# Fixed order and an earlier wait for the first loads of two batches, and a plan with later landings

## The chip, the cores and the metric

The kernel runs on one core of a Trainium2 chip. The metric is the device time of one execution in microseconds (us). A single profiled execution says where time goes, and is itself one draw. Each execution comes with a state, fast or slow (over 1.5% above the fastest of the same kernel, for a kernel on one core).

Names: TensorE (PE in the profile; PEld is its weight load), VectorE (DVE), ScalarE (ACT), GpSimd (POOL), and SyncE (SP), which only issues transfers here. A queue name such as SPq is the engine's instruction queue.

## The reference

Two stages, cut to the mathematics:

```python
# attention: 8 batches, 8 heads, 576 tokens, head size 64, float32
phi(x) = concat(relu(x) * cos_w, relu(x) * sin_w)          # 128 features
kv  = einsum('bhsf,bhsd->bhfd', phi(k), v);  z = phi(k).sum(over s)
num = einsum('bhsf,bhfd->bhsd', phi(q), kv)
den = einsum('bhsf,bhf->bhs', phi(q), z)[..., None] + 1e-6
x   = (num / den)   # as 4608 tokens x 512
# two layers: w_in 512 x 2048, w_out 2048 x 512
h = x @ w_in;  g = h * cos(h);  out = g @ w_out
```

## The kernel before

One Python class, `Plan`, collects steps (engine, cost, data read and written), guesses when each will run, and emits the instructions of each engine in the order of that guess. On the chip the order is fixed and every engine takes its instructions one after the other. A bad guess of when data land therefore makes an engine stand at an instruction whose data are late, with ready work behind it.

The guess for transfers, in the class (cut):

```python
    SHARE, WAKE, LAND = {"HW": 0.42, "SW": 0.58}, {"HW": 1.1, "SW": 1.6}, 1.0
    ...
                for r in on:                    # rings HW (issued by SyncE) and SW (by GpSimd)
                    if rings[r][0][1] < 1e-6:
                        n = rings[r].pop(0)[2]
                        done[n] = now + self.LAND
    ...
                rings[r].append([free[e] + self.WAKE[r], s["dma"][0] / s["dma"][1], n])
```

The transfers of the start. A batch's k, q and v come as float32 through SyncE. The weights come through GpSimd and are cast to float16 on the way. A tiny GpSimd copy (a "hold") that reads one buffer and writes a few elements of another is how one transfer is made to wait for another:

```python
    def weights():
        # hold: w_in waits for batch 0's k
        pl.add("POOL", 0.4, 0.5, 0, hold, hk("k"), [("w_in", g) for g in range(4)])
        for g in range(4):
            ...                                 # w_in, quarter g
        # hold2: w_out waits for w_in's second quarter
        pl.add("POOL", 0.2, 0.3, 0, hold2, [("w_in", 1)], [("w_out", g) for g in range(4)])
        w_out_load(0, 2)                        # first half of w_out

    def hold_raw(nm):                           # batch 1's loads wait for w_out's first quarter
        pl.add("POOL", 0.2, 0.3, 0, lambda: nc.gpsimd.tensor_copy(
            out=raw[nm][0:2, 0, 0, 0:1], in_=w_out_sb[0:2, 0, 0:1]),
            [("w_out", 0)], [((nm, 0), 0), ((nm, 0), 1)])

    def rest_of_w_out():                        # second half of w_out waits for batch 1's q
        ...
        pl.add("POOL", 0.2, 0.3, 0, hold, hk("q"), [("w_out", g) for g in (2, 3)])
        w_out_load(2, 4)

    def second_attention():
        T = start[1] - 30
        for nm, hs in (("k", (slice(0, H),)), ("q", (slice(0, H),)), ("v", HALVES)):
            hold_raw(nm)
            load(1, nm, T, hs)
            if nm == "q":
                rest_of_w_out()
        ...
```

v is loaded in two halves of the heads, but the hold writes only head 0: v's second half is not guarded.

The end of the start-up, in the words used below. Batch 0 goes through attention and layer 1. Then batch 1's attention runs: for each of five groups of tokens a numerator on TensorE, a division on VectorE, a transpose on TensorE, a copy. This is a serial chain. What fills TensorE between its links is layer 2 of batch 0, in eight **filler blocks** of eight 128x512 matmuls, 1.73 us each (`layer2_plain`): four need w_out's first half, four its second. Layer 1 of batch 1 follows.

```python
    def layer2_plain(c):
        ...
        for jh in range(2):                     # half of w_out
            for n, t in enumerate(range(NT) if jh == 0 else (3, 2, 0, 1)):
                ...
                pe(JH, MM, due, mm, [...] + [("w_out", 2 * jh), ("w_out", 2 * jh + 1)], [mk])
```

## Time and profile before

| | before |
|---|---|
| median of the first three executions | 297.37 us (297.03 to 297.64) |
| span of the profiled execution | 295.5 us |
| TensorE issues without a gap from | 140.8 us to 291 us |
| batch 1's hold on GpSimd | 29.0 us |
| first layer-1 matmul of batch 1 | 60.2 us |

Lines of the page of the kernel before. The second and third line cut the span into 40 slices of 7.4 us; a digit is the busy share of TensorE, or its granted clock, in tenths. The last line is the chain that ended last, by engine.

```profile
span 295.5 us, 6280 instructions
...
PE   6768998699999999999999999999999999999994
...
PEclk9977999999999999999999999999999999999999
...
PE 67%; DMA 15%; DVE 9%; ACT 5%; issue 2%; SPq 0%; ACTq 0%; DVEq 0%
```

TensorE is full from the ninth slice on. What can be won lies before it, and the chain names transfers as 15% of the time. The windows view shows where: start and end, length, then busy time and count by engine, the granted clock, the share of the transfer engines and GB/s.

```profile
14.00:26.30 12.30, 8.43 (x105) 6.28 (x103) 7.42 (x28) 5.59 (x12) 1.67 (x3) 0.72 1.21 223
...
42.00:60.00 18.00, 13.41 (x160) 8.48 (x159) 13.58 (x34) 12.06 (x20) 0.00 (x0) 1.00 1.00 259
60.00:141.00 81.00, 79.36 (x773) 57.83 (x771) 76.77 (x160) 62.63 (x103) 0.00 (x0) 1.00 0.96 231
```

From 42 to 60 us TensorE is busy for 13.41 of 18 us: a hole. In the waits view, from 14 to 62 us (us in total, times, longest), these are the waits for late data:

```profile
ACT V L329 <- DMA vm<-in_v_dram: 3.2, 1, 3.2
...
DVE V L332 <- DMA vm<-in_v_dram: 2.9, 1, 2.9
...
DVE kp L319 <- DMA km<-in_k_dram: 2.0, 1, 2.0
...
ACT kp L316 <- DMA km<-in_k_dram: 1.2, 1, 1.2
```

The first two are the unguarded half of v, at 21 to 24 us; the others are batch 2's k, at 51 to 53 us. The timeline of GpSimd: start, length, instruction; in brackets its idle time before and what ended it as far as the profile sees.

```profile
16.19 0.19 POOL L695 COPY w_out_sb<-w_in_sb 1x4 f16<-1x4 f16 x1 [2.93 <-DMA w_in_sb<-in_moe_w_in_dram]
...
29.03 0.18 POOL L708 CAST km<-w_out_sb 2x1 f32<-2x1 f16 x1 [10.87 <-ACT ch L464]
```

The second is batch 1's hold. It waits for w_out's first quarter (the engine named last is only the latest of several that it waits for). The timeline of TensorE over the hole:

```profile
47.14 0.43 PE L404 MATMUL ATT<-kvz,qT 128*128 128x65 f16 x8 [0.79 <-DVE qT L378]
...
47.86 1.89 PE L553 MATMUL M<-w_out_sb,gT 128*128 128x512 f16 x8
49.58 0.42 PE L404 MATMUL ATT<-kvz,qT 128*128 128x65 f16 x8
...
51.22 0.42 PE L404 MATMUL ATT<-kvz,qT 128*128 128x65 f16 x8 [0.33 <-DVE x L424]
52.01 0.38 PE L444 MATMUL M<-IDENT,x 128*128 128x128 f16 x4 [0.37 <-ACT qT L376]
54.69 0.38 PE L444 MATMUL M<-IDENT,x 128*128 128x128 f16 x4 [2.29 <-DVE qT L378]
54.91 1.89 PE L553 MATMUL M<-w_out_sb,gT 128*128 128x512 f16 x8
...
59.75 0.62 PE L444 MATMUL M<-IDENT,x 128*128 128x128 f16 x8 [0.70 <-DVE x L424]
60.21 1.91 PE L491 MATMUL M<-xT,w_in_sb 128*128 128x256 f16 x16
```

L404 are numerators, L444 transposes, L553 a filler block, L491 layer 1.

One more measure is used below, **lost TensorE time**. Take the matmuls' steps from the trace (0.216 us for 128x512, 0.109 us for 128x256, 0.03 to 0.056 us for the small ones), add those issued up to a moment, and subtract from that moment. The sum over the whole kernel is 268.4 us including warm-up matmuls, the same for every kernel here, so what is lost is what differs. A matmul at half clock counts as half lost. Before loses 14.4 us up to 26.3 us, 0.0 from there to 42, 5.6 from 42 to 60, and 2.3 from 60 to 141 us.

### The profile page before, as it was taken

Reading aid. Unit: us, or ns where it says so; the run is one execution under the profiler, and the core shown is the slowest. Engines: PE = TensorE matmul, PEld = TensorE weight load, DVE = VectorE, ACT = ScalarE, POOL = GpSimd, SP = SyncE. Lnnn points to the kernel's source line nnn. Section 1 sums busy time; section 2 is a strip of 40 time slices with the busy share of each in tenths; the row PEclk is TensorE's granted clock in tenths of the full one; section 3 lists DMA queues with packets and bytes.
Section 4 is the critical chain, followed back from the end, with each engine's and each line's share of the span. In section 5 each row is a group of like instructions: output and inputs, shape, how many; then the busy total and the mean of one; then the engine's idle time right before and its main releaser. Section 6 shows DMA issues by size and latency. Waiting matters only on the chain.

```text
span 295.5 us, 6280 instructions
## 1 busy us (share of the span) xinstructions
PE 276.6 (94%) x2460; PEld 194.4 (66%) x2460; DVE 239.3 (81%) x486; ACT 183.6 (62%) x293; POOL 8.9 (3%) x20
## 2 busy tenths in 40 slices
PE   6768998699999999999999999999999999999994
PEld 2446866268977677666766766676668566666783
DVE  2975786798999899988998999999879858665741
ACT  2945895698987756767386849575544554645320
POOL 1520020000000000000000000000000000000000
PEclk9977999999999999999999999999999999999999
DMA  6999979999956999999999939971925100300304
GB/s 214 322 228 213 289 189 257 310 337 191 273 162 157 182 234 250 230 210 297 215 233 298 265 101 241 231 188 46 143 59 170 41 0 2 142 2 1 123 21 142
DMA packets 77565, 53.27 MB, mean 180 GB/s; under 512 B 46048, under 2 KB 75232, under 8 KB 77536
## 3 DMA queue, kind: packets, MB, share of 16 engines
q1 hardware_dynamic: 72592, 48.12, 63.9%
q0 software_dynamic: 4224, 4.19, 8.7%
q10 hardware_dynamic: 720, 0.57, 0.6%
q8 instruction: 19, 0.31, 0.4%
q14 instruction: 10, 0.08, 0.1%
HBM read 36.74 MB, written 9.44 MB: 156 GB/s over the span
## 4 chain that ended last, share of the span: by engine, by line
PE 67%; DMA 15%; DVE 9%; ACT 5%; issue 2%; SPq 0%; ACTq 0%; DVEq 0%
PE M L613 28%; PE M L509 27%; DMA vm<-in_v_dram 7%; PE M L491 6%; DMA qm<-in_q_dram 6%; DVE gT L466 3%; DMA km<-in_k_dram 3%; PE ATT L404 2%; PE ATT L343 2%; ACT ch L464 2%; DVE x L424 1%; PE M L553 1%; ACT kp L316 1%; ACT qp L316 1%; DVE V L332 1%
## 5 line engine op out<-in xcount | busy, mean ns | idle before, releaser
L464 ACT ACTIVATE ch<-M,PIH 128x512 f32<-128x512 f32 x144 | 97.9, 686 | 60.4 <-PE M L509 57.0
L466 DVE TENSOR_TENSOR gT<-M,ch 128x512 f16<-128x512 f32 x144 | 96.8, 685 | 25.8 <-ACT ch L464 24.9
L509 PE MATMUL M<-xT,w_in_sb 128*128 128x512 f16 x384 | 93.8, 379 | 0.0
L613 PEld LDWEIGHTS <-gT 128*128 128x128 f16 x640 | 62.4, 98 | 18.4 <-issue 1.7
L509 PEld LDWEIGHTS <-w_in_sb 128*128 128x128 f16 x448 | 42.1, 98 | 35.0
L613 PE MATMUL M<-w_out_sb,gT 128*128 128x256 f16 x384 | 46.8, 273 | 1.3 <-ACT ost L624 1.3
L491 PE MATMUL M<-xT,w_in_sb 128*128 128x256 f16 x256 | 31.8, 282 | 1.6 <-ACT xT L448 1.6
L613 PE MATMUL M<-T,S 128*128 128x256 f16 x256 | 32.5, 273 | 0.0
L613 PE MATMUL M<-T,gT 128*128 128x256 f16 x256 | 32.2, 273 | 0.0
L613 PEld LDWEIGHTS <-S 128*128 128x128 f16 x256 | 25.1, 98 | 8.0
L491 PEld LDWEIGHTS <-w_in_sb 128*128 128x128 f16 x256 | 25.5, 101 | 5.9 <-issue 2.1
L316 ACT ACTIVATE qp<-qm,CS 128x512 f16<-128x512 f32 x38 | 25.3, 713 | 6.5 <-DMA qm<-in_q_dram 6.5
L316 ACT ACTIVATE kp<-km,CS 128x512 f16<-128x512 f32 x39 | 26.4, 713 | 1.4 <-DMA km<-in_k_dram 1.4
L424 DVE TENSOR_TENSOR x<-ATT,rec 128x512 f16<-128x512 f32 x33 | 22.8, 691 | 1.1
L319 DVE TENSOR_SCALAR qp<-qm,CS 128x512 f16<-128x512 f32 x42 | 18.7, 484 | 5.7 <-DMA qm<-in_q_dram 5.7
L595 DVE TENSOR_TENSOR S<-gT 128x1024 f16<-128x1024 f16 x32 | 21.6, 685 | 0.2
L319 DVE TENSOR_SCALAR kp<-km,CS 128x512 f16<-128x512 f32 x41 | 18.3, 487 | 2.4 <-DMA km<-in_k_dram 2.4
L404 PEld LDWEIGHTS <-qT 128*128 128x128 f16 x320 | 14.7, 98 | 6.3 <-issue 2.7
L404 PE MATMUL ATT<-kvz,qT 128*128 128x65 f16 x296 | 14.8, 194 | 1.6 <-DVE qT L378 0.8
L509 PE MATMUL M<-xR,w_in_sb 128*128 128x512 f16 x64 | 16.1, 379 | 0.0
L332 DVE CAST V<-vm 128x512 f16<-128x512 f32 (+1 forms) x42 | 13.7, 382 | 2.9 <-DMA vm<-in_v_dram 2.9
L343 PEld LDWEIGHTS <-kp 128*128 128x128 f16 x320 | 10.9, 97 | 2.8 <-ACT V L329 1.1
(66 smaller groups left out, 180.2 us busy)
## 6 DMA issues: line engine op xcount, KB each, us to landing
out_dram<-ost SPq DMA_DIRECT2D x33, 256.0 KB, 3.0
qm<-in_q_dram SPq DMA_DIRECT2D x8, 640.0 KB, 6.4
km<-in_k_dram SPq DMA_DIRECT2D x8, 640.0 KB, 5.9
qm<-in_q_dram SPq DMA_DIRECT2D x8, 512.0 KB, 7.0
km<-in_k_dram SPq DMA_DIRECT2D x8, 512.0 KB, 6.7
vm<-in_v_dram SPq DMA_DIRECT2D x6, 640.0 KB, 5.5
vm<-in_v_dram SPq DMA_DIRECT2D x6, 512.0 KB, 5.5
w_in_sb<-in_moe_w_in_dram POOLq DMA_DIRECT2D x4, 512.0 KB, 10.1
```

What stands on the lines that cost most here:

```text
L316: act(0.12 + 0.5 * f, due, lambda: nc.scalar.activation(out=out_, in_=in_, func=AF.Relu, scale=sc), rd, wr)
L319: dve(0.09 + 0.33 * f, due, lambda: nc.vector.tensor_scalar(out=out_, in0=in_, scalar1=0.0, scalar2=sc, op0=ALU.max, op1=ALU.mult), rd, wr)
L332: dve(0.09 + 0.33 * f, due, lambda: nc.vector.tensor_copy(out=out_, in_=in_), rd, wr)
L343: nc.tensor.matmul(bank[hb][:, hh * D1:(hh + 1) * D1], lhsT=kp[:, t, h].rearrange("p g d -> p (g d)"), rhs=V1[:, t, h, :], start=(t == 0), ...
L404: nc.tensor.matmul(bank[hb][:, hh * D1:(hh + 1) * D1], lhsT=a[:, h, :], rhs=z[:, h, :], start=(i == 0), stop=(i == len(parts) - 1))
L424: nc.vector.tensor_tensor(out=split(x16[n][:, hs, :], k), in0=A[:, :, :, 0:D], in1=split(rec[n][:, hs], k).unsqueeze(3).broadcast_to((P, k ...
L464: act(0.59, due, lambda: nc.scalar.activation(out=ch[c], in_=bank, func=AF.Sin, bias=PIH, scale=1.0), [key, "PIH"], [("ch", c)])
L466: dve(0.61, due, lambda: nc.vector.tensor_tensor(out=dst, in0=bank if len(dst.shape) == 2 else bank.rearrange("p (j s) -> p j s", j=dst.sh ...
L491: nc.tensor.matmul(M1[m][:, jj * 2 * P:(jj + 1) * 2 * P], lhsT=w_in_sb[:, cc, j * P:(j + 1) * P], rhs=X[:, cc, ts], start=(cc == 0), stop= ...
L509: nc.tensor.matmul(M1[m], lhsT=w_in_sb[:, cc, j * P:(j + 1) * P], rhs=X[:, cc, :], start=(cc == 0), stop=(cc == NCT - 1))
L595: dve(0.07 + 1.07 / NG, due, lambda: nc.vector.tensor_tensor(out=out_[:, sl], in0=a[:, sl], in1=b[:, sl], op=op), rd, wr)
L613: nc.tensor.matmul(M2[bank][:, tt * MH:(tt + 1) * MH], lhsT=a[:, j, tt * P:(tt + 1) * P], rhs=b[:, j, :], start=(first and tt == 0 and j = ...
```

## The change

The intent is to let batch 1's data come as soon as the first weights have landed, in a fixed order with nothing that cuts in, and to have the plan believe in later landings so that engines do not stand at late data. Core of the diff (cut; the rest carries the new `lane` argument through the plan's forward and backward passes):

```diff
-    SHARE, WAKE, LAND = {"HW": 0.42, "SW": 0.58}, {"HW": 1.1, "SW": 1.6}, 1.0
+    SHARE, WAKE, LAND = {"HW": 0.40, "SW": 0.56}, {"HW": 1.1, "SW": 1.3}, 1.0
+    BUSY, MARGIN = 2.2, 1.0
...
-                        done[n] = now + self.LAND
+                        if r == "SW" and not rings["SW"]:
+                            for x in rings["HW"]:
+                                x[0] = min(x[0], max(now, x[3]))
+                        done[n] = now + self.LAND + (self.MARGIN if now > 13.0 else 0.0)
...
-                rings[r].append([free[e] + self.WAKE[r], s["dma"][0] / s["dma"][1], n])
+                wake = free[e] + self.WAKE[r]
+                late = wake + (self.BUSY if r == "HW" and rings["SW"] and not rings["HW"] else 0.0)
+                rings[r].append([late, s["dma"][0] / s["dma"][1], n, wake])
...
+    ORDER0, ORDER1, HOLDW = "qkv", "kqv", 1
+    GATE1 = (w_in_sb[0:2, 0, Dff // 2 + 1:Dff // 2 + 2], [("w_in", 2)])
...
-            pl.add("SP", 0.65, 0, due, go4, (), [(x, 1 - n) for x in part], dma=(nb * NT, 355.0))
+            pl.add("SP", 0.65, 0, due, go4, (), [(x, 1 - n) for x in part], dma=(nb * NT, 355.0),
+                   lane="first" if b < 2 else None)
...
     def hold_raw(nm):
-        pl.add("POOL", 0.2, 0.3, 0, lambda: nc.gpsimd.tensor_copy(
-            out=raw[nm][0:2, 0, 0, 0:1], in_=w_out_sb[0:2, 0, 0:1]),
-            [("w_out", 0)], [((nm, 0), 0), ((nm, 0), 1)])
+        for h in (0, HB) if nm == ORDER1[2] else (0,):
+            pl.add("POOL", 0.2, 0.3, 0, lambda h=h: nc.gpsimd.tensor_copy(
+                out=raw[nm][0:2, h, 0, 0:1], in_=GATE1[0]),
+                GATE1[1], [((nm, h), 0), ((nm, h), 1)])
```

So there are four parts: the earlier wait (w_in's third quarter instead of w_out's first), the guard on both halves of v, the fixed load order, and the plan's numbers. What the diff does not tell is that the plan, seeing batch 1 wait for w_in's third quarter, loads that quarter first of the four.

More of the change, by code (lines that the diff above doesn't have):

```diff
@@ L36, in __init__, with add @@
         self.steps = []
-        self.wr, self.rd = {}, {}
-    def add(self, eng, occ, lat, due, fn, rd=(), wr=(), dma=None):
+        self.wr, self.rd, self.lanes = {}, {}, {}
+    def add(self, eng, occ, lat, due, fn, rd=(), wr=(), dma=None, lane=None):
         n = len(self.steps)
+        prev = self.lanes.get(lane)
+        if lane is not None:
+            self.lanes[lane] = n
         deps = set()
@@ L55, in add @@
         self.steps.append(dict(eng=eng, occ=occ, lat=lat, due=due, fn=fn,
-                               deps=deps, dma=dma, n=n))
+                               deps=deps, dma=dma, n=n, prev=prev))
         return n
@@ L85, in forward @@
                 users[d].append(s["n"])
+        follow = {s["prev"]: s["n"] for s in st if s["prev"] is not None}
+        left = [k + (s["prev"] is not None) for k, s in zip(left, st)]
         avail, start, done = [0.0] * len(st), [0.0] * len(st), [0.0] * len(st)
@@ L134, in forward @@
             free[e] = t + s["occ"]
+            if n in follow:
+                u = follow[n]
+                avail[u] = max(avail[u], t)
+                left[u] -= 1
+                if not left[u]:
+                    ready[st[u]["eng"]].append(u)
             if s["dma"] is None:
@@ L149, in backward @@
                 left[d] += 1
+            if s["prev"] is not None:
+                left[s["prev"]] += 1
         limit = [end - done[n] + start[n] for n in range(len(st))]
@@ L171, in backward @@
                 limit[d] = min(limit[d], late[n] - self.link(d, n) - (done[d] - start[d]))
+                left[d] -= 1
+                if not left[d]:
+                    ready[st[d]["eng"]].append(d)
+            d = st[n]["prev"]
+            if d is not None:
+                limit[d] = min(limit[d], late[n] - 0.01)
                 left[d] -= 1
@@ L299, in load @@
             nb = len(part) * R * D * 4 / 1e3
-            pl.add("SP", 0.65, 0, due, go4, (), [(x, 1 - n) for x in part], dma=(nb * NT, 355.0))
-            pl.add("SP", 0.65, 0, due, go5, (), [(x, n) for x in part], dma=(nb * (NT + 1), 355.0))
+            pl.add("SP", 0.65, 0, due, go4, (), [(x, 1 - n) for x in part], dma=(nb * NT, 355.0),
+                   lane="first" if b < 2 else None)
+            pl.add("SP", 0.65, 0, due, go5, (), [(x, n) for x in part], dma=(nb * (NT + 1), 355.0),
+                   lane="first" if b < 2 else None)
     def hk(nm, hs=range(H)):
@@ L686, in hold @@
                 out=w_in_sb[0:1, 0, :].rearrange("p (g f) -> p g f", g=4)[:, :, 0],
-                in_=raw["k"][0:1, 0, 0, 0:1].broadcast_to((1, 4)))
-        pl.add("POOL", 0.4, 0.5, 0, hold, hk("k"), [("w_in", g) for g in range(4)])
+                in_=raw[ORDER0[1]][0:1, 0, 0, 0:1].broadcast_to((1, 4)))
+        pl.add("POOL", 0.4, 0.5, 0, hold, hk(ORDER0[1]), [("w_in", g) for g in range(4)])
         for g in range(4):
@@ L707, in hold_raw, with rest_of_w_out @@
     def hold_raw(nm):
-        pl.add("POOL", 0.2, 0.3, 0, lambda: nc.gpsimd.tensor_copy(
-            out=raw[nm][0:2, 0, 0, 0:1], in_=w_out_sb[0:2, 0, 0:1]),
-            [("w_out", 0)], [((nm, 0), 0), ((nm, 0), 1)])
-    def rest_of_w_out():
+        for h in (0, HB) if nm == ORDER1[2] else (0,):
+            pl.add("POOL", 0.2, 0.3, 0, lambda h=h: nc.gpsimd.tensor_copy(
+                out=raw[nm][0:2, h, 0, 0:1], in_=GATE1[0]),
+                GATE1[1], [((nm, h), 0), ((nm, h), 1)])
+    def rest_of_w_out(nm):
         def hold():
@@ L715, in hold @@
                 out=w_out_sb[0:1, JH:, 0].rearrange("p (g j) -> p g j", g=2)[:, :, 0],
-                in_=raw["q"][0:1, 0, 0, 0:1].broadcast_to((1, 2)))
-        pl.add("POOL", 0.2, 0.3, 0, hold, hk("q"), [("w_out", g) for g in (2, 3)])
+                in_=raw[nm][0:1, 0, 0, 0:1].broadcast_to((1, 2)))
+        pl.add("POOL", 0.2, 0.3, 0, hold, hk(nm), [("w_out", g) for g in (2, 3)])
         w_out_load(2, 4)
@@ L724, in first_attention @@
         warm(14, 6.5)
-        for nm, hs in (("q", (slice(0, H),)), ("k", (slice(0, H),)), ("v", HALVES)):
-            load(0, nm, 0, hs)
+        for nm in ORDER0:
+            load(0, nm, 0, HALVES if nm == ORDER0[2] else (slice(0, H),))
         weights()
@@ L745, in second_attention @@
         T = start[1] - 30
-        for nm, hs in (("k", (slice(0, H),)), ("q", (slice(0, H),)), ("v", HALVES)):
+        for nm in ORDER1:
             hold_raw(nm)
-            load(1, nm, T, hs)
-            if nm == "q":
-                rest_of_w_out()
+            load(1, nm, T, HALVES if nm == ORDER1[2] else (slice(0, H),))
+            if nm == ORDER1[HOLDW]:
+                rest_of_w_out(nm)
         for t in range(NT + 1):
```

## The prediction

> **What bounds it now.** TensorE. In the trace's matmul rows successive starts are 0.216 us apart for 128x512, 0.109 us for 128x256. These steps add up to about 263 us outside the warm-ups, in a span of 295.5. From 141 to 291 us it issues without a gap, from 60 to 110 nearly so. Only the early stages can give time: by the same rows about 2.6 us are lost from 22 to 26.3 us, 5.5 us from 42 to 60, 2.3 us from 70 to 141. The first 14 us (batch 0's loads) stay.
>
> **Why these gaps are there.**
> - The waits view: ScalarE waits 3.2 us and VectorE 2.9 us (to 24.4 us) for batch 1's second half of v, a load without a guard. Issued at 14.8 us, its data moved only from 18.6 to 23.2 us, and delayed w_in. Its cast sits ahead of the first cosine on ScalarE, so layer 1 of batch 0 runs freely only from 26.2 us.
> - Batch 1's k and q wait for w_out's first quarter: GpSimd's hold runs at 29.0 us, data flow from 30.5 to 40 us.
> - Batch 2's k is issued at 40.3 us beside w_out's last half and lands near 53 us; VectorE waits 2.0 us and ScalarE 1.2 us for it, with batch 1's copies behind in their queues. Layer 1 of batch 1 starts at 60.2 us.
>
> **What the change does.** No matmul or byte is added, only one GpSimd hold of 0.17 us. The new instruction order (built, not run) puts w_in's third quarter first on GpSimd. So batch 1's hold comes near 16.2 us instead of 29.0, and k, q, v follow in this order, all guarded; the early v load is gone. w_out's first half is issued near 22 us instead of 16.7.
>
> **Estimate of the transfers.** Packet rows: loads alone move about 360 KB/us, weights alone 205 KB/us (written), together about 125 and 115. This agrees with the Trainium skill, "DMA: Bandwidth & Descriptors", Issuing engines are not separate DMA queues: both interleave on the same 16 engines. A load issued beside weights starts 3 to 4 us late. So: w_in complete near 25 us, batch 1's k near 30, q 36, v 40, w_out near 48 (before 50.5), batch 2's k under 51.
>
> **Critical path.** Layer 1 of batch 0: 1.0 us (only part of that gap, as the granted clock is 0.5 from 18.7 to 25.5 us and the idle stretch before it stays). Batch 1's attention and its filler matmuls: 2.4 us. Better estimates of later landings, fewer stalls from 58 to 141 us: 1 us, uncertain, since VectorE is nearly full there (25.8 of 27 us). Sum 4.4 us; a little off for new stalls: **293.3 us, 290.0 to 297.2**. Chances: faster by over 2% 0.22, within 2% 0.75, slower 0.03.
>
> **What would show it.** The waits for v at 21 to 24 us gone; batch 1's first hold near 16 us; layer 1 of batch 0 continuous from about 21.5 us; waits for batch 2's k below 1 us; layer 1 of batch 1 starting at 55 to 57 us; TensorE without gaps from about 137 us to the end.
>
> **What would make it wrong.** Batch 1's k landing after 33 us would stall ScalarE among the cosines of layer 1. The rest of w_in, or w_out's first half, landing later than its matmuls need, since they now share with k and q. The reordered stretch from 100 to 141 us, where VectorE leads, costing or giving 1 to 2 us.

## The result, and the profile after

| | before | after |
|---|---|---|
| median, first comparison | 297.5 us (4 executions) | 292.77 us (4; 292.04 to 293.85) |
| median, repeated on another chip | 296.81 us (11) | 292.73 us (6; 291.68 to 293.96) |
| span of the profiled execution | 295.5 us | 290.6 us |
| TensorE without a gap from | 140.8 us | 136.0 us |

The ratio of the first comparison is 0.9846 (95% interval 0.9811 to 0.9881), of the second 0.9856 (0.9824 to 0.9888). Ratios and intervals here are from the fast executions of the same rounds. They are close to the ratio of the mean times (the largest difference is 0.0013, in the run of the plan's numbers alone), and not quite the ratio of the medians.

The page of the changed kernel:

```profile
span 290.6 us, 6281 instructions
...
PE   7678998999999999998999999999999999999993
...
PEclk9988999999999999999999999999999999999999
...
PE 84%; DMA 7%; DVE 4%; ACT 3%; issue 1%; SPq 0%; DVEq 0%; ACTq 0%
```

The chain has lost half of its share of transfers. The windows:

```profile
14.00:26.30 12.30, 8.94 (x113) 6.79 (x114) 8.80 (x30) 5.75 (x11) 3.23 (x9) 0.86 1.20 228
...
42.00:60.00 18.00, 16.40 (x197) 11.25 (x195) 15.70 (x39) 15.04 (x26) 0.00 (x0) 1.00 1.07 296
60.00:141.00 81.00, 80.20 (x771) 59.06 (x770) 77.96 (x161) 59.23 (x97) 0.00 (x0) 1.00 0.91 225
```

TensorE is busy for 16.40 instead of 13.41 us between 42 and 60 us. By lost time: 13.6 us up to 26.3 us (before 14.4), 0.0 to 42 us (0.0), 2.7 to 60 us (5.6), 1.3 to 141 us (2.3). The differences, 0.8, 2.9 and 1.0, make 4.7 of the 4.8 us by which the gapless stretch starts earlier.

The waits for late data, from 14 to 62 us:

```profile
ACT kp L346 <- DMA km<-in_k_dram: 1.5, 1, 1.5
...
ACT V L359 <- DMA vm<-in_v_dram: 0.7, 1, 0.7
...
DVE V L362 <- DMA vm<-in_v_dram: 0.4, 1, 0.4
```

The 3 us waits for v at 21 to 24 us are gone; batch 2's k still costs ScalarE 1.5 us. GpSimd: batch 1's first hold, and the hold ahead of w_out.

```profile
17.04 0.18 POOL L739 CAST km<-w_in_sb 2x1 f32<-2x1 f16 x1 [2.20 <-DMA w_in_sb<-in_moe_w_in_dram]
...
23.14 0.19 POOL L725 COPY w_out_sb<-w_in_sb 1x4 f16<-1x4 f16 x1 [5.67 <-DMA w_in_sb<-in_moe_w_in_dram]
```

TensorE where the hole was:

```profile
45.85 0.42 PE L434 MATMUL ATT<-kvz,qT 128*128 128x65 f16 x8
...
47.56 0.42 PE L434 MATMUL ATT<-kvz,qT 128*128 128x65 f16 x8 [0.84 <-DVE x L454]
48.15 1.89 PE L583 MATMUL M<-w_out_sb,gT 128*128 128x512 f16 x8 [0.18 <-DVE gT L496]
49.88 0.42 PE L434 MATMUL ATT<-kvz,qT 128*128 128x65 f16 x8
...
50.58 1.89 PE L583 MATMUL TR<-w_out_sb,gT 128*128 128x512 f16 x8
...
52.79 1.89 PE L583 MATMUL M<-w_out_sb,gT 128*128 128x512 f16 x8
...
55.22 1.89 PE L583 MATMUL TR<-w_out_sb,gT 128*128 128x512 f16 x8
56.95 1.91 PE L521 MATMUL M<-xT,w_in_sb 128*128 128x256 f16 x16
```

A filler block (L583) now stands between the links of the chain about every 2.3 us. Layer 1 of batch 1 starts at 56.95 instead of 60.21 us.

### The profile page after: what moved, and what is told of

The parts are those of the page before. It is cut to its first block, busy times and chain, and to the rows that moved or that the text cites. A ratio compares the mean times of both kernels' runs of the same rounds, so it can differ in the third digit from the quotient of the medians.

```text
span 290.6 us, 6281 instructions
## 1 busy us (share of the span) xinstructions
PE 276.6 (95%) x2460; PEld 194.4 (67%) x2460; DVE 239.6 (82%) x486; ACT 182.8 (63%) x293; POOL 9.0 (3%) x21
## 4 chain that ended last, share of the span: by engine, by line
PE 84%; DMA 7%; DVE 4%; ACT 3%; issue 1%; SPq 0%; DVEq 0%; ACTq 0%
PE M L643 33%; PE M L539 33%; PE M L521 7%; DMA vm<-in_v_dram 4%; PE ATT L434 3%; DMA km<-in_k_dram 3%; PE ATT L373 2%; PE M L583 2%; PE TR L583 1%; DVE x L454 1%; DVE kp L349 1%; ACT qp L346 1%; ACT ch L494 1%; PE M L373 1%; PE M L474 1%
## 5 line engine op out<-in xcount | busy, mean ns | idle before, releaser
L494 ACT ACTIVATE ch<-M,PIH 128x512 f32<-128x512 f32 x144 | 98.2, 686 | 66.5 <-PE M L539 56.4
L346 ACT ACTIVATE qp<-qm,CS 128x512 f16<-128x512 f32 x38 | 25.4, 714 | 4.9 <-DMA qm<-in_q_dram 4.9
L625 DVE TENSOR_TENSOR S<-gT 128x1024 f16<-128x1024 f16 x32 | 21.5, 684 | 0.3
L373 PEld LDWEIGHTS <-kp 128*128 128x128 f16 x320 | 11.7, 97 | 3.9 <-ACT V L359 1.3
```

The lines of the kernel that those rows point to most:

```text
L346: act(0.12 + 0.5 * f, due, lambda: nc.scalar.activation(out=out_, in_=in_, func=AF.Relu, scale=sc), rd, wr)
L373: nc.tensor.matmul(bank[hb][:, hh * D1:(hh + 1) * D1], lhsT=kp[:, t, h].rearrange("p g d -> p (g d)"), rhs=V1[:, t, h, :], start=(t == 0), ...
L494: act(0.59, due, lambda: nc.scalar.activation(out=ch[c], in_=bank, func=AF.Sin, bias=PIH, scale=1.0), [key, "PIH"], [("ch", c)])
L625: dve(0.07 + 1.07 / NG, due, lambda: nc.vector.tensor_tensor(out=out_[:, sl], in0=a[:, sl], in1=b[:, sl], op=op), rd, wr)
```

## The experiments

Theory at the start, T: the data of batch 1 and w_out arrive earlier, which pays about 3.4 us, and the plan's numbers pay about 1 us more. Rival P: the better plan pays. Rival V: taking away the early load of v pays. Each kernel was timed in five rounds beside the kernel before on the same chip; four kernels shared a chip and its executions of before. Every result was correct.

The table holds what each run showed. Columns: the time of batch 1's hold; the last packet of its q and of w_out; the start of its first numerator; how many of the eight filler blocks were already spent by then; lost TensorE time from 26.3 to 42, from 42 to 60 and from 60 to 141 us; median and ratio. "Last packet" is the start of the last packet. All but the last two columns are of the one profiled execution. The loss up to 26.3 us is left out: it is 12.3 to 14.5 us in these 14 executions, and the half clock of the start has part in it. All times are in us.

| kernel | hold | q | w_out | first num. | blocks spent | lost 26-42 | lost 42-60 | lost 60-141 | median | ratio (95%) |
|---|---|---|---|---|---|---|---|---|---|---|
| before | 29.0 | 38.3 | 51.7 | 47.1 | 3 | 0.0 | 5.6 | 2.3 | 296.6 to 297.5 | 1 |
| the change | 17.0 | 36.6 | 47.9 | 45.8 | 2 | 0.0 | 2.7 | 1.3 | 292.77 | 0.9846 |
| plan's numbers only | 29.4 | 39.1 | 55.0 | 46.6 | 4 | 0.0 | 6.9 | 0.4 | 297.53 | 1.0019 (0.9984 to 1.0053) |
| old numbers | 16.9 | 36.3 | 47.6 | 45.2 | 2 | 1.6 | 0.1 | 3.6 | 294.70 | 0.9922 (0.9892 to 0.9952) |
| old wait | 28.1 | 37.5 | 48.4 | 48.4 | 4 | 0.0 | 6.9 | 1.6 | 297.88 | 1.0022 (0.9992 to 1.0052) |
| new wait, old order | 18.2 | 37.3 | 47.6 | 47.6 | 3 | 0.5 | 3.6 | 1.9 | 295.66 | 0.9961 (0.9927 to 0.9994) |
| no margin | 17.0 | 36.5 | 48.2 | 45.4 | 2 | 0.4 | 1.6 | 2.6 | 293.48 | 0.9904 (0.9855 to 0.9954) |
| early v, free order | 18.9 | 39.8 | 50.4 | 48.3 | 3 | 2.7 | 5.0 | 1.0 | 297.88 | 1.0017 (0.9986 to 1.0048) |
| late wait, same order | 25.4 | 40.6 | 53.5 | 49.8 | 2 | 4.3 | 1.9 | 1.5 | 297.31 | 1.0011 (0.9981 to 1.0041) |
| the change again | 17.3 | 36.4 | 47.6 | 46.0 | 2 | 0.0 | 3.1 | 1.3 | 292.73 | 0.9856 (0.9824 to 0.9888) |
| w_out late, same order | 16.8 | 36.2 | 52.9 | 46.9 | 2 | 1.4 | 1.9 | 1.8 | 295.35 | 0.9954 (0.9923 to 0.9984) |
| free order | 17.0 | 40.0 | 53.4 | 46.6 | 2 | 2.3 | 2.8 | 0.1 | 293.68 | 0.9896 (0.9865 to 0.9926) |
| quarters in order | 23.0 | 36.6 | 48.8 | 44.0 | 2 | 0.2 | 1.9 | 3.0 | 293.37 | 0.9890 (0.9861 to 0.9919) |
| margin 2 us | 20.0 | 36.6 | 47.7 | 48.1 | 2 | 2.7 | 1.0 | 0.6 | 293.25 | 0.9885 (0.9857 to 0.9914) |

### Only the plan's numbers

The changed kernel with its three other parts put back (cut; the `lane` argument is taken out at both of its places):

```diff
-    GATE1 = (w_in_sb[0:2, 0, Dff // 2 + 1:Dff // 2 + 2], [("w_in", 2)])
+    GATE1 = (w_out_sb[0:2, 0, 0:1], [("w_out", 0)])
-                   lane="first" if b < 2 else None)
+                   lane=None)
-        for h in (0, HB) if nm == ORDER1[2] else (0,):
+        for h in (0,):
```

> The kernel before with nothing new but the plan's numbers and rules for transfers (shares, wake times, the 2.2 us start beside weights, the 1 us margin); batch 1 waits for w_out's first quarter as before, its second half of v is unguarded again and no load order is fixed. Theory T (the data arrive earlier; the plan's numbers are worth about 1 us): 296 to 297 us, ratio to before 0.996 to 1.000, first hold of batch 1 near 29 us. Rival P (the better plan is what pays): 293 to 294.5 us, ratio 0.985 to 0.990, the waits for batch 2's k at 51 to 53 us gone although the data come as late as before.

Measured: 297.53 us, ratio 1.0019. P falls: a plan that believes in later landings, alone, gains nothing. It spends all four blocks of w_out's first half before the first numerator, and the next block comes at 57.9 us. The profiled execution was the fastest of its six (294.94 us), so its stages flatter it.

### The plan's old numbers

```diff
-    SHARE, WAKE, LAND = {"HW": 0.40, "SW": 0.56}, {"HW": 1.1, "SW": 1.3}, 1.0
-    BUSY, MARGIN = 2.2, 1.0
+    SHARE, WAKE, LAND = {"HW": 0.42, "SW": 0.58}, {"HW": 1.1, "SW": 1.6}, 1.0
+    BUSY, MARGIN = 0.0, 0.0
```

> The changed kernel with the plan's old numbers (no margin, no late start, old shares and wake): the transfers are moved, but planned as optimistically as before. T: 293.5 to 294.5 us, ratio 0.986 to 0.990. P: 296 us or more, ratio above 0.995, with waits of VectorE and ScalarE for late loads between 30 and 60 us of 2 us or more.

Measured: 294.70 us, ratio 0.9922: between the two theories. The hole is gone here too, but 3.6 us are lost after 60 us. This is the timeline of TensorE there, in the kernel with the old numbers:

```profile
69.18 0.43 PE L434 MATMUL ATT<-kvz,qT 128*128 128x65 f16 x8 [0.37 <-DMA qT<-qp]
...
71.61 0.43 PE L434 MATMUL ATT<-kvz,qT 128*128 128x65 f16 x8 [1.12 <-DMA qT<-qp]
```

TensorE itself stands at numerators of batch 2 whose transposed q, another transfer, is late. In the changed kernel no wait of TensorE for a transfer is listed in that stretch.

### The old wait

```diff
-    GATE1 = (w_in_sb[0:2, 0, Dff // 2 + 1:Dff // 2 + 2], [("w_in", 2)])
+    GATE1 = (w_out_sb[0:2, 0, 0:1], [("w_out", 0)])
```

> The changed kernel with one thing put back: batch 1's loads wait for w_out's first quarter. Both halves of v stay guarded, order fixed, new plan numbers. First hold of batch 1 near 27 us (no early v beside w_in), q of batch 1 landing near 37 us instead of 34. T: 294.5 to 296 us, ratio 0.990 to 0.995, about half of the gain lost. P: 293 to 293.5 us, as the changed kernel, since the plan knows of the later data. A third theory V (only the early v and its head-of-line wait matter): also as the changed kernel.

Measured: 297.88 us, ratio 1.0022. The whole gain is gone, where T had expected half, and P and V none. Yet most data are hardly later than in the change: q by 0.9 us, w_out by 0.5. Only k is 4.5 us later (33.8 against 29.3), and this kernel first uses it at 37.8 us. No engine but GpSimd waits for a transfer between 14 and 50 us in this trace. The loss is in the order. TensorE of the kernel with the old wait:

```profile
38.48 1.89 PE L583 MATMUL M<-w_out_sb,gT 128*128 128x512 f16 x8
40.20 1.89 PE L583 MATMUL TR<-w_out_sb,gT 128*128 128x512 f16 x8
41.93 1.89 PE L583 MATMUL M<-w_out_sb,gT 128*128 128x512 f16 x8
...
45.15 1.89 PE L583 MATMUL M<-w_out_sb,gT 128*128 128x512 f16 x8
...
48.38 0.42 PE L434 MATMUL ATT<-kvz,qT 128*128 128x65 f16 x8
...
51.73 0.42 PE L434 MATMUL ATT<-kvz,qT 128*128 128x65 f16 x8 [0.66 <-DVE x L454]
...
53.36 0.60 PE L434 MATMUL ATT<-kvz,qT 128*128 128x65 f16 x8 [0.99 <-DVE x L454]
...
55.18 0.61 PE L474 MATMUL M<-IDENT,x 128*128 128x128 f16 x4 [0.80 <-DVE x L454]
...
56.04 3.60 PE L583 MATMUL M<-w_out_sb,gT 128*128 128x512 f16 x8
```

Told of the later wait, the plan put batch 1's preparation behind nearly all of layer 1 of batch 0, and all four first-half blocks ahead of the first numerator. The chain then runs with no filler block between its links from 48.4 to 56.0 us. Neither the weights nor the gates forced this: the next block needs w_out's second half, whose last packet came at 48.4 us, and gates of batch 0, the last of which VectorE ended at 43.6 us; the block stands in the order at 56.04. It takes 3.60 instead of 1.89 us: after the thin stretch the clock was granted at half from 53.3 to 60.1 us.

### The new wait in the old order

The kernel before, with one source changed; no engine's order moves:

```diff
-            out=raw[nm][0:2, 0, 0, 0:1], in_=w_out_sb[0:2, 0, 0:1]),
+            out=raw[nm][0:2, 0, 0, 0:1], in_=w_in_sb[0:2, 0, Dff // 4 + 1:Dff // 4 + 2]),
```

> The kernel before, every engine's order of instructions unchanged, but batch 1's hold reads w_in's first-landing quarter instead of w_out, so the hold runs right after w_out's descriptors at about 18.5 us and not at 29. The early v stays first in the load queue. T: data earlier, batch 2's k lands 2 us earlier or more, 295 to 296.5 us, ratio 0.991 to 0.997. P: without a new plan nothing is gained: 297 to 298 us, ratio 0.998 to 1.003, the engines reach the same instructions at the same times and wait elsewhere.

Measured: 295.66 us, ratio 0.9961, as T expected. Earlier data alone, with every instruction where it was, give about 1 us, a quarter of the change.

These four runs gave a second theory, T2: the earlier wait removes the hole, and the plan's numbers keep the later stalls small.

### No margin

```diff
-    BUSY, MARGIN = 2.2, 1.0
+    BUSY, MARGIN = 2.2, 0.0
```

> The changed kernel with one number of the plan put back: no 1 us margin on landings after 13 us; the late start beside weights, the shares, the order and the wait for w_in stay. Theory T2 (formed after the first four runs: the earlier wait for w_in removes the hole of TensorE from 50 to 60 us, and the plan's numbers, the margin above all, then keep later stalls small): hole from 50 to 60 us stays gone (under 0.5 us), stalls of 1 to 2 us come back between 60 and 141 us, 293.5 to 295 us, ratio 0.988 to 0.993. Rival L (the late-start rule and shares, not the margin): as the changed kernel, ratio near 0.985.

Measured: 293.48 us, ratio 0.9904, against 0.9856 of the change in the same rounds. The intervals overlap, so the time alone doesn't settle it. The trace agrees with T2: no loss from 50 to 60 us, and 2.6 instead of 1.3 us from 60 to 141 us.

### Early v and a free order

```diff
-                   lane="first" if b < 2 else None)
+                   lane=None)
-        for h in (0, HB) if nm == ORDER1[2] else (0,):
+        for h in (0,):
```

> The changed kernel without the guard on the second half of v and without the fixed order of loads: v's second half comes early again beside w_in; wait for w_in's third quarter and plan numbers stay. T2: the guard and the order are worth little once batch 1 starts at 17 us: ratio 0.985 to 0.990, hole from 50 to 60 us under 1 us. Rival V (the early v delays w_in and blocks ScalarE, and its removal is what pays): ratio 0.993 or more, waits for v of about 3 us at 21 to 24 us again.

Measured: 297.88 us, ratio 1.0017. T2 was wrong to hold this part cheap. The plan also makes another order without these two, so it isn't the data alone that differ. v's second half is again the first load (issued at 15.2 us), k lands at 35.5 us and q at 39.8. The predicted sign of V, a wait for v of 3 us, is not in this trace, where v is cast later. Instead ScalarE waits 3.2 us for k between the cosines of layer 1.

### A late wait in the same order

The changed kernel, all orders unchanged, with the hold reading the quarter of w_in that lands last:

```diff
-                out=raw[nm][0:2, h, 0, 0:1], in_=GATE1[0]),
+                out=raw[nm][0:2, h, 0, 0:1], in_=w_in_sb[0:2, 0, 3 * Dff // 4 + 1:3 * Dff // 4 + 2]),
```

> The changed kernel with every engine's instruction order unchanged, but batch 1's hold reads the quarter of w_in that lands last, so k starts about 7 us later than planned (hold near 24 to 25 us instead of 17). T2 (time of data): k lands 3 to 5 us later, q and v 2 to 3 us later; ScalarE stalls in the cosines near 33 us for 1 to 3 us, part of the hole before 60 us returns: 294.5 to 296.5 us, ratio 0.990 to 0.997. Rival O (the order of instructions is what pays): within 1 us of the changed kernel.

Measured: 297.31 us, ratio 1.0011, more than T2 expected. Rival O falls: the new order without the data in time is worth nothing. (The late hold stands in GpSimd's queue ahead of w_out's first half, so it also makes the weights late: w_out's last packet comes at 53.5 instead of 47.9 us. The run does not part this from the late k.) In the waits of this kernel, 14 to 62 us:

```profile
ACT kp L346 <- DMA km<-in_k_dram: 4.6, 2, 2.5
...
DVE kp L349 <- DMA km<-in_k_dram: 3.7, 2, 3.1
```

Both engines stand at batch 1's k, which the order has put among the cosines and gates of layer 1; TensorE loses 4.3 us between 26 and 42 us, where the change loses nothing.

### The change again

> The changed kernel itself, for comparison on the same chip in the same rounds: 292 to 294 us, ratio 0.982 to 0.988, no TensorE hole from 50 to 60 us.

Measured: 292.73 us, ratio 0.9856. The result repeats on another chip, and the second trace has the same stages as the first.

### w_out late in the same order

```diff
-                out=w_out_sb[0:1, JH:, 0].rearrange("p (g j) -> p g j", g=2)[:, :, 0],
-                in_=raw[nm][0:1, 0, 0, 0:1].broadcast_to((1, 2)))
+                out=w_out_sb[0:2, JH:, 0].rearrange("p (g j) -> p g j", g=2)[:, :, 0],
+                in_=raw["v"][0:2, HB, 0, 0:1].broadcast_to((2, 2)))
```

> The changed kernel, the order of instructions on every engine unchanged, but the hold ahead of w_out's second half reads the third piece of batch 1's v instead of q, so that half starts later (hold near 39 us instead of 34, last weight packets near 52 us instead of 48). Theory W (the earlier end of w_out pays, since it gives TensorE filler matmuls): 294.5 us or more, ratio 0.990 or more, TensorE waits for w_out near 53 us. Theory B (batch 1's k, q, v arriving early pays; w_out has slack: its second half is first used at 52.8 us in the changed kernel): within 0.7 us of the changed kernel, ratio 0.983 to 0.988.

Measured: 295.35 us, ratio 0.9954: over 2 us of the gain lost, as W expected. But the trace does not show W's sign. w_out ends at 52.9 us, the first block that needs it starts at 53.9, and no wait of TensorE for it is listed. What this trace lost against the change (1.6 us up to 141 us) it had lost by 42 us (1.9 us), under a half clock that lasted from 18.9 to 29.1 us, before the edit can act. The profiled execution was also the fastest of the six (294.0 us). So the loss in time is measured and its path is open; that a block with its weights landing within 1 us of its start sometimes waits would fit, and was not seen.

### Free order, v guarded

```diff
-                   lane="first" if b < 2 else None)
+                   lane=None)
```

> The changed kernel without the fixed order of the first loads; both halves of v stay guarded, wait for w_in's third quarter and plan numbers stay. The plan then loads batch 1 as k, v, q. It parts the two things that the run with the early v took away together. If the early, unguarded v was the loss: ratio 0.984 to 0.989. If the order was (q last holds up the q transposes and, through GpSimd, w_out's second half): q lands near 39 us instead of 34, ratio 0.992 to 1.000, TensorE's hole before 60 us back with 2 us or more. I hold the second for likelier.

Measured: 293.68 us, ratio 0.9896 (five fast executions; the slow one is left out), between the two answers offered. It parts the run with the early v: putting back the guard alone, with the order that the plan then makes, takes the ratio from 1.0017 to 0.9896 (on two chips, each against before), so the guard on v's second half is the larger part. The fixed order is worth about 0.5%, which is not clear of noise (0.9896 against 0.9846 and 0.9856, in other rounds, with overlapping intervals). q does land late (40.0 us) and TensorE loses 2.8 us from 42 to 60 us, as I held likelier, but that costs less than I thought. The sum hides a shift: the change loses its 2.7 us before 50 us and nothing from 50 to 60, this kernel the reverse. It has a hole again, though only two blocks were spent before the first numerator.

### w_in's quarters in their natural order

```diff
             pl.add("POOL", 0.9, 0, 0, lambda fs=fs: nc.gpsimd.dma_start(
-                out=w_in_sb[:, :, fs], in_=wi[:, :, fs]), (), [("w_in", g)], dma=(1048.0, 400.0))
+                out=w_in_sb[:, :, fs], in_=wi[:, :, fs]), (), [("w_in", g)], dma=(1048.0, 400.0), lane="w_in")
```

> The changed kernel with w_in's quarters loaded in their natural order 0, 1, 2, 3, so the third quarter, for which batch 1 waits, is third and not first. The plan knows this. Hold of batch 1 near 23 to 25 us, q near 37 us. Theory B: most of the gain is lost, ratio 0.992 to 1.002, as with the wait for w_out. If only a wait on anything in w_in mattered, not how early it lands: ratio 0.984 to 0.989.

Measured: 293.37 us, ratio 0.9890. Theory B, that the early landing of batch 1's data is what pays, is wrong in the size: with the hold at 23.0 us most of the gain stays. Set beside the old wait this is the most telling pair. k's last packet comes at 33.7 us in this kernel and 33.8 in that one, q at 36.6 and 37.5, w_out at 48.8 and 48.4; their times are 293.37 and 297.88 us. With nearly the same data, the order differs: two blocks spent before the first numerator at 44.0 us here, four before the first at 48.4 us there.

```profile
35.10 1.89 PE L583 MATMUL M<-w_out_sb,gT 128*128 128x512 f16 x8
...
38.57 1.89 PE L583 MATMUL M<-w_out_sb,gT 128*128 128x512 f16 x8
...
43.98 0.42 PE L434 MATMUL ATT<-kvz,qT 128*128 128x65 f16 x8 [0.59 <-ACT kvz L390]
```

Not all of the 4.5 us is the order's. The mean clock of the six executions was 0.994 here and 0.977 there. In the profiled executions (5.6 us apart) 1.7 us of the difference had come by 26.3 us, before any of these blocks (12.3 against 14.0 us lost; here no half clock at the start, there one of 6.8 us); 5.0 us came from 42 to 60 us, and from 60 to 141 us this kernel lost 1.4 us more than the other.

### A margin of 2 us

```diff
-    BUSY, MARGIN = 2.2, 1.0
+    BUSY, MARGIN = 2.2, 2.0
```

> The changed kernel with a margin of 2 us instead of 1 us on later landings; all else as in the change. It shows whether the margin has a smooth optimum or merely shuffles the order of instructions. Smooth: 0 us gave a ratio of 0.990, 1 us 0.986, so 2 us 0.984 to 0.988. Shuffle: anything from 0.983 to 0.995, with stalls in another stage than without margin (there they were at 70 to 100 us).

Measured: 293.25 us, ratio 0.9885. By its time it is not apart from the change. By its stages it is another kernel: 2.7 us lost from 26 to 42 us and 0.6 after 60, where without a margin it was 0.4 and 2.6. The margin is not a smooth knob: it shuffles the order. No run beat the changed kernel, so none is offered in its place.

## Why the prediction was right, and where it was not

The time (293.3 us predicted, 292.77 measured) and the stages were right. Lost TensorE time in the two profiled executions, by the terms of the prediction's sum:

- **Layer 1 of batch 0, 1.0 us predicted; 0.8 measured** (14.4 to 13.6 us lost up to 26.3 us). The sign named for it failed: layer 1 was not continuous from 21.5 us but from 25.4, because the new order puts batch 0's last numerator behind the first layer-1 matmuls (VectorE waits 2.7 us for it). In this execution the half clock lasted 3.4 us instead of 6.8, so part of the 0.8 us may be the clock's. The waits for v did go, but the guard is not needed for that: the kernel with only the plan's numbers keeps the early v, casts it on ScalarE from 26.1 us, lists no wait for it, and lost 12.7 us up to 26.3 us, less than the change. So the agreement of 0.8 with 1.0 is in part luck.
- **Batch 1's attention and its filler matmuls, 2.4 us predicted; 2.9 measured** (5.6 to 2.7 us lost from 42 to 60 us). Layer 1 of batch 1 starts at 56.95 us (55 to 57 predicted).
- **Fewer stalls from 58 to 141 us, 1 us predicted; 1.0 measured** (2.3 to 1.3 us lost from 60 to 141 us). The gapless stretch starts at 136.0 us (137 predicted).
- **Transfers.** Predicted and last packet measured: w_in 25 and 27.1 us, batch 1's k 30 and 29.3, q 36 and 36.6, v 40 and 42.5, w_out 48 and 47.9, batch 2's k under 51 and 49.2. Batch 1's first hold came at 17.0 us (16.2). That both kinds share the same 16 engines, for which the prediction cites the Trainium skill, shows in the packet rows: with both queues active, loads moved 120 to 133 KB/us and weights 116 to 128 (in steps of 1 us).
- **Waits for batch 2's k below 1 us: wrong.** ScalarE waits 1.5 us for it.

What failed is the step that took these gains as separate sums, earlier data 3.4 us and better estimates 1 us. The runs show parts that do not add:

- Earlier data in the old order: ratio 0.9961. The plan's numbers alone: 1.0019. All but the plan's numbers: 0.9922. All together: 0.9846 and 0.9856. With the other parts in place the plan's numbers are worth about 0.7%; alone, nothing.
- With the new order and late data nothing is left (1.0011). With the old wait, hence an order planned for it, nothing is left either (1.0022).
- The guard on v's second half, 1.2% with the order free (1.0017 to 0.9896, with the new plan that comes with it), was in the prediction only as a part of the 1.0 us of the first stage. Mis-sized.

What goes with a hole is how many filler blocks are spent before batch 1's first numerator: three or four in the five that lost 3.6 to 6.9 us between 42 and 60 us, two in the nine that lost 0.1 to 3.1 us there. The kernel with the late wait is among the nine and slow: it had lost its time before. The two groups lie close (3.1 and 3.6 us), and from 50 to 60 us alone they overlap: the free order lost 2.8 us there with two blocks spent, the new wait in the old order 2.6 with three. So the count tells the large holes (4.6 to 6.1 us from 50 to 60 us, in four kernels with three or four blocks) and not the small ones. Two rivals for the large holes can be set aside. A late first numerator does not make one: with two blocks spent it came at 48.1 and 49.8 us, and 1.0 and 1.4 us were lost from 50 to 60; with four it came at 46.6 us, and 4.9 were lost. Nor do late weights: w_out's last packet came at 48.4 us with the old wait, which lost 6.1 us from 50 to 60, and at 52.9 us in the run with w_out late, which lost 0.1. The prediction named the filler matmuls in half a line; they turned out to be central to the account. That the number of blocks is a cause, and not only a companion of the slow kernels, was shown by no run that moved the blocks alone, though the pair with nearly equal data (old wait, quarters in order) leaves little else between 42 and 60 us but the half clock on the hole.

Part of the difference goes with the clock. Over the 108 fast executions with a recorded clock, within one kernel and call the time fell by about 0.9 us for each 0.01 of mean granted clock (fitted over all, correlation -0.53). The kernel before had a mean clock of 0.985 in its 33 executions, the changed kernel 0.992 in ten; by the fit the 0.007 stand for about 0.6 of the some 4 us gained. The Trainium skill, "TensorE: Matmul & The Clock Gate", Part 1: The HAM clock gate, says that the clock is halved after an idle window of about 3.4 us, that the windows run freely, and that their position varies by run. In lengths and places the traces agree: the half-clock stretches here are 3.4, 6.8 or 10.2 us long and start elsewhere in each. But none followed an idle window: before each of the 20 stretches ahead of 280 us TensorE was busy for 1.0 to 2.1 of the last 3.4 us, 1.4 us of it in the old wait's hole (49.9 to 53.3 us). A thin chain was enough. In three kernels with a hole one lies on it (plan's numbers only 54.2 to 57.6 us, old wait 53.3 to 60.1, early v 56.4 to 59.8); in the two profiled executions of the change there is none after the start. The profiled execution before had none there either, so how much of the 0.007 of clock the hole costs on average stays open.

## What to carry to other kernels

When engines run fixed orders, independent filler work is a stock to be spent between the links of a serial chain: look at how much of it is left when the chain starts (here a companion of the large holes, not a shown cause), and not only at when the data land. Earlier data and a plan that knows of them are one change; measured apart, each showed a quarter of the gain or none. Time the repeats and read the granted clock beside each before explaining a difference below 1%.

## What the Trainium skill lacked or had wrong

- "DMA: Bandwidth & Descriptors", Latency and other measured facts, gives about 600 ns to the first byte of a transfer issued by SyncE. Beside running weights it was 3.9 us here (batch 1's k issued at 17.25 us, first packet at 21.15), and in the kernel before 3.9 us for batch 2's k (40.3 to 44.2). At the end of the weights it was 1.4 us (29.2 to 30.6). The page does not tell of this delay.
- The same page, Queues, rings and completion order, says that each engine alternates between queues at packet granularity. It gives no rate for a casting weight transfer beside plain loads: 116 to 128 KB/us (written) for the weights and 120 to 133 KB/us for the loads here, against about 205 and 360 alone.
- "TensorE: Matmul & The Clock Gate", Part 1, says that the penalty of the ramp, the slow clock at the start of matmul work, is below 1% of a typical kernel span. That is no bound on what the clock costs between executions: here mean clocks from 0.970 to 1.000 were seen, and 0.01 goes with about 0.9 us of 295, so that range is about 0.9%, as large as most of the differences between these kernels. And the idle window that it names was not needed: a stretch with TensorE busy 1.0 to 2.1 of 3.4 us came before each of the 20 half clocks ahead of 280 us.
